# Talking-heads attention and a squared-ReLU FFN on one core: near copies ranked last, output matmuls in twos, and the left-over lines of the first batch as chunks of their own

## The chip, the cores and the metric

The kernel runs on one NeuronCore of a Trainium2 chip. The engines are named as in the profile: PE (TensorE, matrix multiply), DVE (VectorE), ACT (ScalarE), POOL (GpSimd) and SP (SyncE, which here only issues transfers). The metric is the device time of one execution in microseconds (us). All times before are of the kernel as it stood; the medians are over three runs.

## What is computed

Eight batches, twelve heads, 448 positions, head dimension 64. The scores of all heads are mixed across heads with a 12x12 matrix before the softmax, and the attention weights are mixed again with another one after it. The result, 3584 rows of 768, goes through an FFN with a squared ReLU.

```python
def _attn_ref(q, k, v, w_pre, w_post):              # q, k, v: (8, 12, 448, 64)
    scores = scale * np.matmul(q, k.transpose(0, 1, 3, 2))
    scores = np.einsum('bhij,hg->bgij', scores, w_pre)
    scores = scores - np.max(scores, axis=-1, keepdims=True)
    attn = np.exp(scores)
    attn = attn / (np.sum(attn, axis=-1, keepdims=True) + 1e-09)
    attn = np.einsum('bhij,hg->bgij', attn, w_post)
    return np.matmul(attn, v)

def _moe_ref(x, w_in, w_out):                       # x: (3584, 768), w_in: (768, 2048)
    h = np.maximum(x @ w_in, 0.0)
    return h * h @ w_out
...
    x = np.ascontiguousarray(attn_out.transpose(0, 2, 1, 3)).reshape(B * S, H * D)
    return _moe_ref(x=x, **moe_kwargs)
```

## The kernel before

**Order.** No loop issues the instructions directly. The program first describes its work as operations (`add`: an engine or a choice of engines with an assumed cost, a rank `pri`, a function that issues the instructions, what it depends on, a PSUM bank that it takes). `Planner.run` then plays the operations through an event list with those costs; each free engine takes the ready operation of lowest rank. The order that comes out is the program: each engine has a fixed list, and waits at its head for the semaphores of what that instruction needs. A wrong cost changes no result, only the order. The assumed costs are constants of the code, such as `NEAR` (L39), `load` (L498) and `first` (L1029). Ranks are counted in chunks: chunk n has rank n, and what must be ready for it has n minus some lead (`AHEAD`, L43). FFN operations have the rank `FILL` = 1e6, so they fill what attention leaves open. Where PE would stand idle early on, the planner inserts matmuls on a tile of zeros (`still`, L1183; the rule is in L234 with `IDLE_LOW`).

**One batch of attention.** The 448 query positions are cut into four blocks: r = 0 is the tail, the last 64 positions; r = 1, 2, 3 are three interleaved sets of 128 out of the first 384. Per batch:

1. q and k are transposed. In batches 0 and 1 PE does that (`t_qk`, L547). From batch 2 on (`x_piece`, L612) a *near copy* brings the heads next to each other (`pair_k`, `pair_q`, L616 to L620, into `kn` and `qn`; 3 + 3 copies for each half of the heads, on POOL or DVE as the planner chooses), and a DMA transpose issued by SP turns them into `kt` and `qz` (L623, L629). `kn` and `qn` exist once, so the second half's copies wait for the first half's transposes.
2. Scores (`score`, L679): one matmul of 448 columns for each head, two heads beside each other on half the rows of PE for r > 0, and one matmul for a pair of heads for the tail. They are evacuated by DVE or ACT (L485, L487, the `copy` helper) into one of two buffers `snat`.
3. A *relay* (`relayout`, L707) is a DMA issued by SP from `snat` to `sch`, which gathers 10 positions of 12 heads into 120 lines of 448: a *chunk*. There are 45 in a batch. The blocks' 128 positions are not a multiple of ten: eight lines of each are left over, and are put together with left-over lines of the block before it. `schl` is a buffer for one such chunk of 96 lines, whose first 24 come from the tail and whose other 72 from block 2.
4. For each chunk (`chunk`, L761): the mix (L801, PE, one matmul with the mixing matrix), the maximum (L812, DVE), the exponential with its sum (L815, ACT), the reciprocal for two chunks (L821, DVE), the second mixing matrix scaled by it (`wq`, L824, POOL), four matmuls that mix, transpose and normalise at once (`at`, L831, PE), and their evacuation into `atb` (L485 or L487).
5. When a block's chunks are through, `av` (L876) multiplies with v, and the result goes to `xt`, which holds the FFN input of two batches. The FFN runs on units of 128 or 256 positions (`unit`, L916): the first matmul (L933), ReLU (L947 on DVE, L951 on ACT), square (L954, POOL), the output matmuls (L972), their evacuation to `osb` (L989), the store (L996). An operation of the output matmuls is four of the 16 steps of a sum (L969).

**Batch 0 differs.** Block 1 comes first, as *direct* chunks: no score is stored and relayed. Instead DVE multiplies q with the fanned-out mixing matrix (`f_prep`, L790, into `osb`, not used by then), and six matmuls over the head pairs (L807) give the mixed scores at once. The places of the chunks are in `ORDER0` (L72): block 1's twelve whole chunks (7 to 18), its left-over chunk 6 (which includes the tail's lines), the tail's chunks 0 to 5, then 19 to 44. Chunk 19 is the one in `schl`, chunk 32 mixes left-over lines of blocks 2 and 3. `TAIL_FIRST` (L83) sets when the tail's scores are due. The tail's scores of batch 0 are stored in the second `snat` (L656), which block 3 uses later; L684 makes block 3's scores wait for the tail's relays.

**Queues.** SP issues all relays, all DMA transposes and nearly all stores, in order. POOL issues the loads (L350, L356, L361, L1068, L1074), between its `wq`, squares and near copies.

## Time and profile before

| | |
|---|---|
| median of three runs | 581.34 us (580.34 to 581.96) |
| the profiled execution | 582.53 us |
| its span, first to last instruction | 580.8 us |
| granted PE clock, mean | 0.997 |
| exponentials (L815, ACT) | x360, 641 ns each |
| maxima (L812, DVE) | x360, 610 ns each |
| first FFN matmul (L933), 128x256 and 128x128 | x1632, 164.3 us busy |
| output matmul (L972) | x912, 173.0 us busy |
| `wq` (L824, POOL) | x347, 123.6 us busy |
| near copies on DVE (L610) | 19 of k, 9.2 us; 16 of q, 6.5 us |
| near copies on POOL (L610) | 17 of k, 10.2 us; 20 of q, 10.5 us |

The profile is of one execution. Busy times of an engine are unions of its instructions' times; the ends of matmuls are modelled, so a matmul's own duration overlaps that of the next, and a busy PE is not PE at its peak. The page has 40 slices of 14.5 us: DVE is at eight tenths or more in all but the first and the last three, and the DMA engines are at nine tenths in the first four slices and at one or two tenths in the last.

### The profile page before, as it was taken

To read this page: it belongs to the slowest core of one execution; us is meant where nothing else is said; L and a number is where in the kernel's file an instruction comes from. 1 tells how busy PE (TensorE), PEld (TensorE's weight loads), DVE (VectorE), ACT (ScalarE), POOL (GpSimd) and SP (SyncE) were. 2 spreads that over 40 slices of the span, in tenths; PEclk is the share of its full clock that TensorE was granted. 3 is DMA by queue.
4 is the path that set the end of the run, shared out by engine and by line. 5 is a ranking of instruction groups with operands and counts; after the bars stand their busy time and mean duration, and the time that the engine had idled before them with its cause. 6 is when DMAs were issued, how large, how long until landed. Compare 5 with 4: busy or idle time off the path is not lost.

```text
span 580.8 us, 16782 instructions
## 1 busy us (share of the span) xinstructions
PE 566.0 (97%) x5820; PEld 406.4 (70%) x5820; DVE 507.6 (87%) x1124; ACT 452.4 (78%) x1198; POOL 323.0 (56%) x593
## 2 busy tenths in 40 slices
PE   7989999999999898999999999999999999999997
PEld 4667666776677576767668677767768676767785
DVE  7999998999989899989898998999899988988442
ACT  5789989789888876888897888889798888887200
POOL 8357356655665267635776357734677344645441
PEclk9999999999999999999999999999999999999999
DMA  9999849954897449764498649954297545322021
GB/s 136 217 186 220 164 114 197 159 146 125 155 157 169 136 120 182 158 133 122 92 204 144 158 142 143 199 131 133 76 201 160 153 139 113 118 75 80 2 56 54
DMA packets 131810, 80.90 MB, mean 139 GB/s; under 512 B 59298, under 2 KB 126732, under 8 KB 131724
## 3 DMA queue, kind: packets, MB, share of 16 engines
q1 hardware_dynamic: 84892, 56.99, 40.1%
q0 software_dynamic: 46784, 22.81, 30.3%
q8 instruction: 45, 0.74, 0.5%
q14 instruction: 41, 0.34, 0.2%
q10 hardware_dynamic: 48, 0.02, 0.0%
HBM read 45.61 MB, written 11.01 MB: 98 GB/s over the span
## 4 chain that ended last, share of the span: by engine, by line
PE 84%; DMA 5%; DVE 5%; POOL 3%; issue 2%; ACT 1%; DVEq 0%; SPq 0%; POOLq 0%
PE bank L933 24%; PE bank L972 22%; PE bank L831 12%; PE bank L801 10%; PE bank L876 6%; PE bank L679 6%; DMA ks<-in_k_dram 2%; DMA sch<-snat 2%; DVE mn L812 1%; PE bank L807 1%; DVE atb L485 1%; DMA qs<-in_q_dram 1%; POOL wq L824 1%; DVE snat L485 1%; POOL ks L361 1%
## 5 line engine op out<-in xcount | busy, mean ns | idle before, releaser
L815 ACT ACTIVATE es<-bank,mn 120x448 bf16<-120x448 f32 x360 | 228.0, 641 | 50.5 <-DVE mn L812 45.7
L824 POOL TENSOR_SCALAR wq<-wback,rc 120x120 bf16<-120x120 f32 (+1 forms) x347 | 123.6, 369 | 158.1 <-DVE rc L821 93.7
L812 DVE TENSOR_REDUCE mn<-bank 120x1 f32<-120x448 f32 x360 | 209.2, 610 | 2.0 <-PE bank L801 1.8
L972 PE MATMUL bank<-w,h 128*128 128x384 bf16 (+2 forms) x912 | 173.0, 323 | 0.0
L933 PE MATMUL bank<-xt,w 128*128 128x256 bf16 (+1 forms) x1632 | 164.3, 253 | 0.8 <-ACT es L815 0.7
L954 POOL TENSOR_TENSOR h<-hr 128x512 bf16<-128x512 f32 x112 | 116.5, 1041 | 66.0 <-DVE hr L947 37.0
L933 PEld LDWEIGHTS <-w 128*128 128x128 bf16 x1632 | 136.1, 98 | 24.5 <-issue 3.9
L831 PEld LDWEIGHTS <-es 120*112 120x112 bf16 (+1 forms) x1440 | 107.9, 130 | 31.9 <-ACT es L815 6.3
L485 DVE CAST atb<-bank 112x480 bf16<-112x480 f32 (+2 forms) x188 | 114.6, 617 | 13.6 <-PE bank L831 11.6
L831 PE MATMUL bank<-wq,es 120*112 120x120 bf16 (+1 forms) x1440 | 118.3, 217 | 5.8 <-POOL wq L824 3.5
L972 PEld LDWEIGHTS <-h 128*128 128x128 bf16 x912 | 85.8, 97 | 54.1 <-issue 2.1
L487 ACT CAST atb<-bank 112x480 bf16<-112x480 f32 (+3 forms) x196 | 103.0, 538 | 12.0 <-PE bank L831 10.1
L801 PE MATMUL bank<-sch,wmix 120*128 120x448 bf16 x339 | 107.0, 354 | 0.7 <-DVE atb L485 0.5
L485 DVE CAST snat<-bank 128x448 bf16<-128x448 f32 x152 | 88.8, 613 | 3.6 <-PE bank L679 1.5
L487 ACT CAST snat<-bank 128x448 bf16<-128x448 f32 x172 | 84.4, 543 | 4.6 <-PE bank L679 3.3
L815 ACT ACTIVATION_READ_ACCUMULATOR es<-bank,mn 120x1 f32 x360 | 74.1, 206 | 0.0
L947 DVE TENSOR_SCALAR hr<-bank 128x512 f32<-128x512 f32 x80 | 55.0, 688 | 18.5 <-PE bank L933 15.1
L801 PEld LDWEIGHTS <-wmix 120*128 120x128 bf16 (+1 forms) x347 | 30.9, 98 | 21.4 <-issue 12.7
L876 PE MATMUL bank<-atb,vs 112*64 112x192 bf16 (+3 forms) x864 | 40.4, 250 | 0.0
L679 PE MATMUL bank<-kt,qz 64*128 64x448 bf16 x276 | 39.0, 357 | 0.8 <-DVE hr L947 0.6
L876 PEld LDWEIGHTS <-vs 112*64 112x64 bf16 x864 | 36.4, 110 | 3.4 <-issue 2.5
L485 DVE COPY osb<-bank 128x384 f32<-128x384 f32 (+2 forms) x32 | 17.3, 541 | 21.3 <-PE bank L972 18.2
(72 smaller groups left out, 307.1 us busy)
## 6 DMA issues: line engine op xcount, KB each, us to landing
sch<-snat SPq DMA_DIRECT2D x324, 105.0 KB
out_dram<-osb SPq DMA_DIRECT2D x22, 360.0 KB
vs<-in_v_dram POOLq DMA_DIRECT2D x16, 336.0 KB, 8.3
ks<-in_k_dram POOLq DMA_DIRECT2D x14, 336.0 KB, 9.5
qs<-in_q_dram POOLq DMA_DIRECT2D x14, 288.0 KB, 9.9
w<-in_moe_w_in_dram POOLq DMA_DIRECT2D x6, 512.0 KB, 14.6
w<-in_moe_w_out_dram POOLq DMA_DIRECT2D x4, 768.0 KB, 19.6
out_dram<-osb SPq DMA_DIRECT2D x8, 192.0 KB
```

What stands on the lines that cost most here:

```text
L485: nc.vector.tensor_copy(out=out_, in_=in_)
L487: nc.scalar.copy(out=out_, in_=in_)
L679: nc.tensor.matmul(slot[:, 0:S], lhsT=lhsT, rhs=kt[i][half, :, at_, :], start=True, stop=True)
L801: nc.tensor.matmul(slot[:, 0:S], lhsT=wm[0:rows, :], rhs=src[0:rows, :], start=True, stop=True,)
L812: nc.vector.tensor_reduce(out=mn[i][0:rows, :], in_=slots[mk][0:rows, 0:S], axis=AX.X, op=ALU.min)
L815: nc.scalar.activation(out=es[i][0:rows, 0:S], in_=slots[mk][0:rows, 0:S], func=ACT.Exp, scale=-1.0, bias=mn[i][0:rows, 0:1], accum_out=sm ...
L824: nc.gpsimd.tensor_scalar(out=wq[i][0:rows, :, 0:ns], in0=back[0:rows, :, 0:ns], scalar1=rc[i // 2][0:rows, i % 2:i % 2 + 1], scalar2=1.0, ...
L831: nc.tensor.matmul(slot[0:P_KEYS, jb * H * ns:(jb + 1) * H * ns], lhsT=es[i][0:rows, jb * P_KEYS:(jb + 1) * P_KEYS], rhs=wq[i][0:rows, :, ...
L876: nc.tensor.matmul(v_[64 * hh:64 * hh + 64, i, 0:x1 - x0], lhsT=vs[:, 2 * c2 + hh, jb, :], rhs=atb[half][:, jb, 2 * c2 + hh, x0:x1], start ...
L933: nc.tensor.matmul(slot[:, j * w:(j + 1) * w], lhsT=w1[c2][:, (f0 + j) * 128:(f0 + j + 1) * 128], rhs=xt[:, c2, a:z], start=(c2 == 0), sto ...
L954: nc.gpsimd.tensor_tensor(out=h2_[:, f0:f0 + nf, 0:w], in0=hr[gi % 2][:, :].rearrange("p (f c) -> p f c", f=nf), in1=hr[gi % 2][:, :].rear ...
L972: nc.tensor.matmul(slot[:, 0:c1 - c0], lhsT=h2_[:, ft, mt * 128:(mt + 1) * 128], rhs=w2[:, ft, c0:c1], start=(ft == 0), stop=(ft == FT - 1),)
```

## The change

Five things, and constants of the plan.

- *Near copies rank last.* `pair_k` and `pair_q` get the rank 2e6, behind everything else, and other assumed costs (POOL 640 ns where it was 1000, DVE 480 where it was 270).
- *Output matmuls in twos.* An operation of L972 is two of the 16 steps (`OSTEP`), not four, and costs half in the plan.
- *Left-over lines of batch 0 apart.* Chunk 6 keeps the left-over lines of block 1 and the tail, chunk 19 now holds those of block 2 and the tail and becomes direct like chunk 6, ahead of the tail's chunks; chunk 32 holds block 3's alone (96 lines). `schl` is no longer used in batch 0. 14 direct chunks, not 13.
- *Tail scores of batch 0 in `xt`*, in the half that batch 1 fills later: block 3's scores no longer wait for the tail's relays. Instead batch 1's evacuations to `xt` wait for them (`old += relay_of[0]`), and batch 1's k and q slots wait for the tail scores' matmuls (`used`). The tail's scores are due by their own chunk's place, not by `TAIL_FIRST`.
- *AV earlier in the program of batch 0*: blocks 0 and 2 are given to `av` behind their last whole chunk (`C0[1] - 1`, `C0[3] - 1`).
- Constants: `AHEAD` 7.4 to 7.0, `IDLE_LOW` 0.55 to 0.62, a load's issue 750 to 830 ns, and the assumed times of the first loads (k 48 to 52, q 36 to 42, tail 24 to 30 ns a row).

```diff
 NSLOT = 2
-NEAR, TURN_SP = {"POOL": 1000, "DVE": 270}, 1500
+NEAR, TURN_SP = {"POOL": 640, "DVE": 480}, 1500
 PIECE = NPAIR // 2
...
 NSCH = 11
-AHEAD = 7.4
+AHEAD = 7.0
 FIFO = 50
-IDLE_NS, IDLE_COLS, IDLE_FROM, IDLE_END, IDLE_LOW = 112, 256, 1300, 130000, 0.55
+IDLE_NS, IDLE_COLS, IDLE_FROM, IDLE_END, IDLE_LOW = 112, 256, 1300, 130000, 0.62
 SPELL, PHASE, DROP, RISE = 3413, 1700, 0.4, 0.8
...
 LATER = 2
+NEAR_LAST = 2e6
+OSTEP = 2
 GS, ONE = [(0, 1, 2)], [(0,), (1,), (2,)]
...
 UNITS0 = [(0, 128), (128, 256), (256, 384), (384, 640), (640, 896)]
-ORDER0 = [*range(C0[1] + 1, C0[2]), C0[1], *range(C0[1]), *range(C0[2], NCHUNK)]
+EARLY = 6
+ORDER0 = [*range(C0[1] + 1, C0[2]), C0[1], C0[2], *range(EARLY), *range(C0[2] + 1, C0[3]), *range(EARLY, C0[1]), *range(C0[3], NCHUNK)]
 NQW = 4
...
 TAIL0, Q0 = 19, 0.7
-TAIL_FIRST = 8
 
...
             deps = list(deps) + [loads[-7]]
-        op = add("POOL", 750, pri, fn, deps, lat=850)
+        op = add("POOL", 830, pri, fn, deps, lat=850)
         done = pl.moved("LOAD", rows, each[0], each[1], 0, [op], 1500)
...
         i = 2 * b + piece - NSLOT
-        far = prep_op + [m_op[n] for n in direct] if b == 1 else []
+        far = prep_op + [m_op[n] for n in direct] + [score_ops[0, 0, p] for p in range(NPAIR)] if b == 1 else []
         return far + [score_ops[i // 2, NJ, PIECE * (i % 2) + x] for x in range(PIECE)] if i >= 0 else []
...
         ck = [
-            add(NEAR, 0, pri, lambda eng, a=a: pair_k(eng, a), [k_in[b, g], tk_op.get(2 * b + g - 1)], lat=80)
+            add(NEAR, 0, NEAR_LAST, lambda eng, a=a: pair_k(eng, a), [k_in[b, g], tk_op.get(2 * b + g - 1)], lat=80)
             for a in range(PIECE)
...
         cq = [
-            add(NEAR, 0, pri, lambda eng, a=a: pair_q(eng, a), [q_in[b, g], tq_op.get(2 * b + g - 1)], lat=80)
+            add(NEAR, 0, NEAR_LAST, lambda eng, a=a: pair_q(eng, a), [q_in[b, g], tq_op.get(2 * b + g - 1)], lat=80)
             for a in range(PIECE)
...
     def store_of(b, r):
-        return snat[1 if b == 0 and r == 0 else r % 2]
+        return xt[:, :, S:W2B] if b == 0 and r == 0 else snat[r % 2]
 
...
     def is_direct(b, c):
-        return b == 0 and C0[1] <= c < C0[2]
+        return b == 0 and C0[1] <= c <= C0[2]
 
...
 
-        first = TAIL_FIRST if b == 0 and r == 0 else C0[r]
+        first = min(place_of(b, c) for c in range(C0[r], (C0 + [NCHUNK])[r + 1]) if not is_direct(b, c)) - b * NCHUNK
         pri = b * NCHUNK + first - AHEAD - 0.6 - (0.7 if r == 0 else 1.4) * (NPAIR - p)
         n = b * (NJ + 1) + r - 2
-        old = list(relay_of.get(n if n != 1 else 0, [])) if n else []
+        old = list(relay_of.get(n, [])) if n > 1 else []
         ins = [op for p_ in group for op in ready[b, p_][r]] + ([ready_tail[b, p]] if r == 0 else [])
...
             parts = [(blk, 0, KC, sn[2 * CI * cc:2 * CI * (cc + 1), 0:NPAIR, :])]
+        elif b == 0 and cc == 0:
+            parts = [(blk, 0, 96, sn[120:P, :, :])]
         elif cc == 0:
...
             relay_of.setdefault(of, []).append(move(n, pri, ns, deps + old, src_of[n][r0:r1, :], srcs, lat))
-        if r == 0 and cc == 5:
+        if r == 0 and cc == 5 and b > 0:
             here.append(move(
...
             return [(half, base + CI * (cc - 1), 0, CI)]
+        if b == 0 and r > 1:
+            return [(0, rest + 62, 0, 2), (1, 120, 2, 8)] if r == 2 else [(1, P_ROWS + 120, 0, 8)]
         return [
...
         r, cc = block_of(c)
-        rows = 96 if c == C0[2] else KC
+        rows = 96 if c == C0[2 if b else NJ] else KC
         ns = rows // H
...
             for lo, hi, first, x, s0, step, w in (
-                ([(64 * x_, 64 * x_ + 64, 0, zt, P - 8 + x_, 2, 2) for x_ in range(2)] if cc == 0 else []) +
+                ([(64 * x_, 64 * x_ + 64, 0, zt, P - 8 + 4 * (r - 1) + x_, 2, 2) for x_ in range(2)] if cc == 0 else []) +
                 [(0, P, PIECE * i_, qz[i_], CI * (cc - 1) if cc else P_ROWS - 8, 1, CI if cc else 8) for i_ in range(2)]
...
                     o = 2 if w == 8 else 0
-                    src_ = x[lo:hi, 0, :, s0:s0 + w] if size < NPAIR else x[lo:hi, :, s0:s0 + step * (w - 1) + 1:step]
+                    src_ = x[lo:hi, r - 1, :, s0:s0 + w] if size < NPAIR else x[lo:hi, :, s0:s0 + step * (w - 1) + 1:step]
                     (nc.vector if eng == "DVE" else nc.gpsimd).tensor_tensor(
...
         old = []
+        if b == 1:
+            old += relay_of[0]
         if b >= 2:
...
                 key = ("f", ix, "o", mt, nt)
-                for f0 in range(0, FT, 4):
+                for f0 in range(0, FT, OSTEP):
                     def mms(slot, f0=f0, mt=mt, c0=c0, c1=c1):
-                        for ft in range(f0, f0 + 4):
+                        for ft in range(f0, f0 + OSTEP):
                             nc.tensor.matmul(
...
                     if f0 == 0:
-                        prev = add("PE", 12 + (c1 - c0) * 5 // 3, fill + 20 + 4 * mt + 2 * nt, keep(key, mms),
-                                   [prev] + sq_op[ix][0:4 // nf] + w2_in[0:1 if ix < SOON else 4], lat=0, bank=key)
+                        prev = add("PE", (12 + (c1 - c0) * 5 // 3) * OSTEP / 4, fill + 20 + 4 * mt + 2 * nt, keep(key, mms),
+                                   [prev] + sq_op[ix][0:max(1, OSTEP // nf)] + w2_in[0:1 if ix < SOON else 4], lat=0, bank=key)
                     else:
-                        prev = add("PE", 12 + (c1 - c0) * 5 // 3, FILL, lambda key=key, mms=mms: mms(slots[key]), [prev, w2_in[f0 // 4]] + sq_op[ix][0:(f0 + 4) // nf], lat=0)
+                        prev = add("PE", (12 + (c1 - c0) * 5 // 3) * OSTEP / 4, FILL, lambda key=key, mms=mms: mms(slots[key]), [prev, w2_in[f0 // 4]] + sq_op[ix][0:(f0 + OSTEP + nf - 1) // nf], lat=0)
                     o_op[ix].append(prev)
...
         if what[0] == "k":
-            k_in[0, what[1]] = first(us, 28, 48)
+            k_in[0, what[1]] = first(us, 28, 52)
         elif what[0] == "a":
...
         elif what[0] == "q":
-            q_in[0, what[1]] = first(us, 32, 36)
+            q_in[0, what[1]] = first(us, 32, 42)
         elif what[0] == "t":
-            tails0.append(first(us, 24, 24))
+            tails0.append(first(us, 24, 30))
     tail_in[0] = add("TAIL", 0, 0, lambda: None, tails0, lat=0)
...
                 unit(0, 0)
-            if c == C0[2]:
+            if c == C0[1] - 1:
                 for gs in ONE:
                     av(0, 0, gs, P_ROWS, XA)
-            if c == C0[3]:
+            if c == C0[3] - 1:
                 for gs in ONE:
```

## The prediction

> **What bounds the kernel now.** I read the busy times of the page first, then the busy time by stage, then what ended TensorE's (PE's) waits, and last the order of time around the longest of them.
>
> ```profile
> span 580.8 us, 16782 instructions
> PE 566.0 (97%) x5820; PEld 406.4 (70%) x5820; DVE 507.6 (87%) x1124; ACT 452.4 (78%) x1198; POOL 323.0 (56%) x593
> ```
>
> PE is busy 97% of the span, so the time is PE's work plus the little that it idles: 580.8 − 566.0 = 14.8 us. The stages tell where that is (columns: length, then busy us of PE, weight load, DVE, ACT, POOL, then clock, DMA share, GB/s):
>
> ```profile
> 16.00:33.00 17.00, 16.93 (x117) 11.97 (x116) 16.78 (x48) 11.95 (x32) 4.93 (x11) 1.00 1.05 208
> 33.00:55.00 22.00, 20.38 (x333) 15.30 (x332) 20.55 (x50) 20.65 (x56) 17.30 (x30) 1.00 1.25 205
> 55.00:68.00 13.00, 11.26 (x163) 7.41 (x162) 13.00 (x32) 12.05 (x35) 4.05 (x11) 1.00 0.98 184
> ...
> 150.00:240.00 90.00, 86.38 (x868) 61.14 (x863) 83.13 (x178) 72.31 (x196) 56.16 (x103) 1.00 0.88 159
> 240.00:540.00 300.00, 299.98 (x3007) 216.53 (x3005) 271.93 (x589) 253.52 (x675) 169.53 (x318) 1.00 0.63 134
> 540.00:581.00 41.00, 37.02 (x319) 27.72 (x316) 13.61 (x24) 2.30 (x6) 12.10 (x13) 1.00 0.14 40
> ```
>
> From 240 to 540 PE never idles: there, a reordering moves the end only if it changes PE's own work. Up to 68 us it is VectorE (DVE) that is full (16.78 of 17.00, 13.00 of 13.00), and the FFN has little to give PE. So time can be won in three places: the first 68 us, 150 to 240 us (3.6 us of PE idle), and the last 4 us, a closing evacuation and store that the edit leaves alone. What ended PE's waits after the first minute:
>
> ```profile
> PE bank L831 <- POOL wq L824: 1.6, 2, 0.9
> PE bank L831 <- DVE osb L485: 1.6, 1, 1.6
> PE bank L933 <- ACT es L815: 0.7, 1, 0.7
> PE bank L679 <- DVE hr L947: 0.6, 1, 0.6
> ```
>
> The 0.6 and the 0.7 are one event. In order of time:
>
> ```profile
> 225.36 0.60 POOL L610 COPY kn<-ks 112x512 bf16<-112x512 bf16 x1
> 226.03 2.38 DVE L610 COPY kn<-ks 112x512 bf16<-112x512 bf16 x1
> 227.20 1.05 POOL L954 TENSOR_TENSOR h<-hr 128x512 bf16<-128x512 f32 x1
> 229.45 0.37 PE L679 MATMUL bank<-kt,qz 64*128 64x448 bf16 x2 [0.63 <-DVE hr L947]
> 231.36 1.47 PE L933 MATMUL bank<-xt,w 128*128 128x256 bf16 x12 [0.69 <-ACT es L815]
> ```
>
> One near copy took 2.38 us on DVE, where the median of its kind is 0.295 (the tile's view), while GpSimd (POOL) worked without a break from 225.36 to 228.25; the DVE work queued behind it then held PE.
>
> **The change, part by part.** The sum is made against the profiled execution: 582.53 us, of which the span is 580.8. The median of the runs is 581.34, so 1.19 is taken off at the end.
>
> *One more direct chunk in batch 0.* Block 2's left-over lines become a direct chunk: six matmuls for one. Twelve direct matmuls took 2.44 us (at 29.96) and six took 1.30 (at 33.20), so 0.19 each: PE gains 5 × 0.19 = 0.95. DVE gets four more preparations (L790): two of 64x144 at 0.300 and two of 128x288 at 0.295, together 1.19. Both fall where PE (16.93 of 17.00) and DVE are full. Against it, one evacuation piece of `atb` falls away and 21 fewer KB are relayed. Bounds: 0 if a hole swallows it, +1.2 if DVE pays all. I take +0.9, near the full price, as that stage has no holes. Five more standing matmuls (39 to 44) fill holes of PE by construction: 0. The cover is a wait that is there anyway; without it they would cost 5 × 0.11 = 0.6 (half of the 0.213 of one at the half clock of the start).
>
> *Left-over lines apart, tail scores in `xt`.* Block 3's scores no longer wait for the relays of the tail, which held the same buffer; block 2 is complete after its twelfth relayed chunk, one chunk before the mixed chunk with block 3. So the AV matmuls of the second unit, which started at 66.05, can start a chunk earlier: 42 maxima began between 17.7 and 69.9, so (69.9 − 17.7) / 41 = 1.27 us. What it can win are PE's holes from 55 to 68: 13.00 − 11.26 = 1.74, and the five standing matmuls just before that AV (0.65). Bounds: 0, if DVE, full there, sets the pace anyway, and −2.4. I take −1.2, one chunk.
>
> *The start.* Load costs are raised in the plan, so the order now puts scores between the transposes of q, where PE idled 0.67 and 1.07 us for q. Block 2's twelve score matmuls all stand ahead of the first direct chunk (eight before) and five of the six tail scores behind it. The first maximum still needs all of q and its preparations. Bounds −1.7 and 0; I take −0.4, as the loads set the pace.
>
> *Near copies rank last.* In the built order DVE has 19 of them, 35 before; POOL 53, 37 before. The 35 on DVE took 9.2 + 6.5 = 15.7 us (groups of L610), against 35 × 0.29 = 10.2 at the median: some 5.5 us are such blocked time, and 16/35 of it goes. POOL gets 8 × 0.61 + 8 × 0.55 = 9.3 us more, and stays under 60%. Each copy's transposes still stand 12 and more chunks ahead of the scores that need them, so lateness costs nothing. Worth to PE: the event at 226 cost 0.63 + 0.20 + 0.69 = 1.52; DVE's other delays are hidden under FFN matmuls. Bounds −2.5 (with half of DVE's 5.5 × 16/35 = 2.5 reaching PE early, at 150 to 240) and +1.0 (two POOL waits of the 0.9 kind return before `wq`). I take −1.5.
> [...]
>
> *FFN output in pieces of two.* The matmuls are the same, 880 of 384 columns in the group with the most forms; a filler lasts 0.33 us rather than 0.65. Entries into the scores' half-row mode go from 70 to 71 in the built order, so switching costs nothing new. Mixes followed at once by their `at` (the pair in which PE waits for `wq`) go from 40 to 32, and the pieces fill such gaps. The holes it can reach: 0.91 at 79.21, 0.45 at 167.91, 1.58 at 198.07. Bounds −2.9 and +0.7 (a delay of 0.1 at each of seven more score-to-filler changes). The 1.58 hangs on an output store that DVE and ACT wait for, which no piece of PE shortens; I take −1.0.
>
> *The constants* (AHEAD, IDLE_LOW, load costs) act through the order above: 0.
>
> Sum: 0.9 − 1.2 − 0.4 − 1.5 − 1.0 = −3.2; 582.53 − 3.2 = 579.3 for a profiled run, and 579.3 − 1.2 = 578.1 against the median.
>
> **The rivals.**
> *Nothing is won* (0.14). DVE paces the first 68 us with as much work as before, the w2 loads keep the first output matmuls back to 80.5 us whatever comes before, and the holes at 79, 168, 198 and 229 reappear elsewhere, as such holes belong to any plan that is off by a microsecond. For it: DVE at 13.00 of 13.00. Against it: the near copy at 226 has a cause that the change addresses. Left are 0.9 of cost and about 1.3 of gain: 580.9.
> *The relays of batch 0 come late: slower* (0.21). Before, all six tail scores were evacuated ahead of the first maximum, their relays issued from 17.6, 0.8 us apart, for a first use at 32.23. Now the last tail score stands behind the second pair of `at`, which ended at 24.66 + 0.59 = 25.25; the six relays wait for its evacuation, to about 26, and block 2's twelve queue behind them on SyncE, to about 26 + 18 × 0.8 = 40.4. The DMA engines are full here (share 1.05, 1.25). The queue's view gives the relays' pace: from 22 to 31, beside the w1 loads, 467 packets of theirs, and from 32 to 35, with those loads landed, 643 (columns: packets, MB, share of the engines):
>
> ```profile
> q1 hardware_dynamic: 467, 0.39, 16.8%
> ...
> q1 hardware_dynamic: 643, 0.53, 53.5%
> ```
>
> A relay is 120 lines, so 2.3 us there and 0.56 us here. The tail's own relays are still in time: the first, behind loads for 3.4 us as before (issued 17.57, no packet from 17 to 21), lands near 26 + 3.4 + 2.3 = 31.7, and its use moves one direct chunk on, to 32.23 + 1.27 = 33.5. But they take the fast stretch from 32 to 35 that was block 2's, and block 2's then fall among batch 1's loads of q and k, issued from 32.89. Block 2 is needed from 33.5 + 6 × 1.27 = 41. It decides when the pace among those loads falls to that beside w1: twelve times 2.3 us from 35 end at 62.6, against a use of the last at 41 + 12 × 1.27 = 56. If half of that delay of 6 stands as a hole of ACT, DVE and PE together (the FFN matmuls of the first unit fill some), 3 us are lost, and with the direct chunk and half of the other gains the run ends at 581.34 + 3 + 0.9 − 2.0 = 583.2. For it: the load of the engines. Against it: without relays beside them the w1 loads end sooner, by about 0.39 MB at 211 GB/s, 1.8 us, and the bytes are the same.
> *It does more than said*: all holes within reach close (start −1.7, AV −2.4, near copies −2.5, pieces −2.9) and the direct chunk costs 0.9: −8.6, 572.7. It is the low end of the forecast's case.
>
> **How the numbers follow.** What a measurement of this kernel can tell is about 0.3%, 1.7 us: faster is below 579.6, slower above 583.1. The forecast's case, the closing of more holes in it, holds 0.65, with its own range 573 to 580.5; almost all of it counts as faster. Nothing won: 0.14. Late relays: 0.21, nearly all of it above 583.1, as its price is open upwards. So faster 0.64, same 0.17 (with the upper edge of the forecast's case and the lower one of the late relays), slower 0.19. The range of 573 to 585 takes in both other cases and leaves out the closing of every hole and a hole of over 5 us.
>
> **What would show it.** Right: no near copy over 1.5 us on DVE with a PE wait behind it around 226; the second unit's AV before 65.5; PE idle from 150 to 240 under 2 us; output matmuls in twos between an `es` and its `at`. The direct chunk shows as 84 direct matmuls, and as a first relayed mix later than 32.2. Wrong: a hole of PE, DVE and ACT together between 33 and 60, ended by a relay into `sch` (the late relays); PE idle as large as before with new releasers (nothing won); a wait of `at` for `wq` behind near copies on POOL. If PE idles again after 240, a premise has fallen that all the cases share.

## The result, and the profile after

| | before | after |
|---|---|---|
| median, eight runs each beside each other | 582.70 us (580.34 to 585.48) | 578.40 us (577.92 to 580.14) |
| after / before | | 0.9913, 95% interval 0.9887 to 0.9939 |
| the profiled execution, its span | 582.53, 580.8 | 577.99, 576.2 |

The recorded ratio times 582.7 is a gain of 5.1 us (3.6 to 6.6), where 3.2 was forecast; the forecast's own ratio, 578.1 / 581.34 = 0.9944, lies just above the interval. (581.34 was the median of the first three of the eight runs before.) The recorded ratio is not the quotient of the two medians, which is 0.9926, a gain of 4.3; this text goes by recorded ratios throughout. The page of the changed kernel:

```profile
span 576.2 us, 16829 instructions
PE 565.1 (98%) x5830; PEld 407.5 (71%) x5830; DVE 510.2 (89%) x1124; ACT 445.9 (77%) x1185; POOL 329.4 (57%) x609
```

Its stages (columns as in the prediction: length, busy us of PE, weight load, DVE, ACT, POOL, clock, DMA share, GB/s):

```profile
12.00:16.00 4.00, 3.83 (x35) 1.97 (x34) 3.99 (x14) 4.00 (x11) 2.67 (x5) 1.00 1.37 198
...
33.00:55.00 22.00, 21.48 (x334) 16.28 (x332) 20.80 (x52) 20.25 (x58) 16.39 (x29) 1.00 1.23 199
55.00:68.00 13.00, 12.38 (x198) 9.24 (x198) 13.00 (x33) 11.57 (x34) 5.00 (x12) 1.00 0.95 179
...
90.00:150.00 60.00, 59.08 (x628) 43.24 (x625) 56.10 (x123) 47.88 (x128) 34.31 (x68) 1.00 0.76 145
150.00:240.00 90.00, 88.87 (x894) 63.40 (x895) 86.98 (x183) 73.34 (x199) 59.36 (x108) 1.00 0.88 163
240.00:540.00 300.00, 298.98 (x3036) 217.73 (x3033) 272.84 (x585) 251.15 (x668) 173.45 (x328) 1.00 0.65 135
```

The start of the kernel before, the same stage:

```profile
12.00:16.00 4.00, 3.88 (x30) 2.10 (x29) 3.64 (x13) 3.61 (x9) 2.57 (x5) 0.57 1.39 202
```

Length less PE's busy time gives its idle time in each stage of the two profiled executions:

| PE idle, us | 0 to 33 | 33 to 90 | 90 to 150 | 150 to 240 | 240 to 540 | 540 to the end | all |
|---|---|---|---|---|---|---|---|
| before | 3.0 | 4.3 | 0.1 | 3.6 | 0.0 | 3.8 | 14.8 |
| after | 2.9 | 1.2 | 0.9 | 1.1 | 1.0 | 3.9 | 11.1 |

So 5.5 us of holes went, 3.0 in batch 0's attention and FFN start and 2.5 between 150 and 240, and 1.8 came back elsewhere. Idle falls by 3.7 and the span by 4.6. The last 0.9 is in busy time. The clock from 12 to 16 was 0.57 before and is 1.00 now, which is worth an estimated (1.00 − 0.57) × 4 = 1.7 us of PE's work; against it stand the five added direct matmuls, 0.9. All of this is of one execution of each kernel.

What ended PE's waits in the changed kernel (columns: us in total, times, longest):

```profile
PE bank L807 <- DVE snat L487: 2.0, 2, 1.1
PE bank L1191 <- DVE still L369: 1.1, 1, 1.1
```

The waits of `at` for `wq` (L824 before, L830 now) are gone from its lines; before, there were five between 33 and 68 us alone:

```profile
PE bank L831 <- POOL wq L824: 2.6, 5, 0.8
```

In order of time, what the prediction asked to see in batch 0; first the kernel before, then the changed one:

```profile
32.23 0.35 PE L801 MATMUL bank<-sch,wmix 120*128 120x448 bf16 x1
...
66.05 1.53 PE L876 MATMUL bank<-atb,vs 112*64 112x128 bf16 x48
```

```profile
30.77 1.35 PE L813 MATMUL bank<-kt,osb 128*120 128x448 bf16 x6
...
35.29 0.35 PE L807 MATMUL bank<-sch,wmix 120*128 120x448 bf16 x1
...
62.76 1.53 PE L882 MATMUL bank<-atb,vs 112*64 112x128 bf16 x48
...
77.17 0.49 PE L980 MATMUL bank<-w,h 128*128 128x384 bf16 x2
```

The added direct chunk stands at 30.77. The first relayed mix is 3.1 later than before (32.23), and yet the AV of the second unit is 3.3 earlier (66.05) and the first output matmul too (80.50), which goes out as a piece of two. And the event that was to vanish, a near copy on DVE kept out by POOL, is still there, at another place:

```profile
166.25 2.90 DVE L612 COPY qn<-qs 128x384 bf16<-128x384 bf16 x1
...
166.95 2.04 POOL L962 TENSOR_TENSOR h<-hr 128x512 bf16<-128x512 f32 x2
...
169.08 0.60 DVE L487 CAST snat<-bank 128x448 bf16<-128x448 f32 x1
...
169.73 0.92 PE L807 MATMUL bank<-sch,wmix 120*128 120x448 bf16 x3 [1.11 <-DVE snat L487]
```

The copy ends at 169.15, 0.16 after POOL's squares (168.99), as the one at 226 did before; the evacuation behind it on DVE is late, and PE waits 1.11. DVE's near copies are 19 now (35 before), three of them over 1 us (five before). Together they take 7.1 + 5.2 = 12.3 us. Less 19 × 0.29 = 5.5, as the prediction counted, that leaves 6.8 us in which they are kept out, where it was 5.5 before: there are fewer copies on DVE, but no less of this time.

### The profile page after: what moved, and what is told of

The parts are those of the page before. It is cut to its first block, busy times and chain, and to the rows that moved or that the text cites. A ratio compares the mean times of both kernels' runs of the same rounds, so it can differ in the third digit from the quotient of the medians.

```text
span 576.2 us, 16829 instructions
## 1 busy us (share of the span) xinstructions
PE 565.1 (98%) x5830; PEld 407.5 (71%) x5830; DVE 510.2 (89%) x1124; ACT 445.9 (77%) x1185; POOL 329.4 (57%) x609
## 4 chain that ended last, share of the span: by engine, by line
PE 87%; DVE 6%; DMA 3%; ACT 2%; issue 1%; POOL 0%; DVEq 0%; ACTq 0%; POOLq 0%
PE bank L980 24%; PE bank L941 23%; PE bank L837 12%; PE bank L807 11%; PE bank L882 7%; PE bank L681 6%; DMA sch<-snat 3%; PE bank L813 2%; DVE mn L818 1%; DVE atb L487 1%; DVE snat L487 1%; PE bank L1191 1%; ACT es L821 1%; DVE qn L612 1%; ACT snat L489 0%
## 5 line engine op out<-in xcount | busy, mean ns | idle before, releaser
L830 POOL TENSOR_SCALAR wq<-wback,rc 120x120 bf16<-120x120 f32 (+1 forms) x346 | 123.0, 367 | 148.4 <-DVE rc L827 90.3
L980 PE MATMUL bank<-w,h 128*128 128x384 bf16 (+2 forms) x912 | 184.1, 323 | 0.0
L837 PEld LDWEIGHTS <-es 120*112 120x112 bf16 (+1 forms) x1440 | 110.9, 129 | 27.7 <-ACT es L821 3.7
L837 PE MATMUL bank<-wq,es 120*112 120x120 bf16 (+1 forms) x1440 | 120.8, 217 | 0.5 <-ACT es L821 0.2
L980 PEld LDWEIGHTS <-h 128*128 128x128 bf16 x912 | 83.7, 98 | 51.7 <-issue 5.2
L487 DVE CAST atb<-bank 112x480 bf16<-112x480 f32 (+3 forms) x184 | 112.9, 622 | 7.8 <-PE bank L837 4.9
L489 ACT CAST atb<-bank 112x480 bf16<-112x480 f32 (+3 forms) x199 | 103.8, 537 | 19.1 <-PE bank L837 18.3
L807 PE MATMUL bank<-sch,wmix 120*128 120x448 bf16 (+1 forms) x339 | 108.2, 354 | 2.6 <-DVE snat L487 2.0
L489 ACT CAST snat<-bank 128x448 bf16<-128x448 f32 x165 | 81.8, 546 | 7.7 <-PE bank L681 7.2
L955 DVE TENSOR_SCALAR hr<-bank 128x512 f32<-128x512 f32 x75 | 51.6, 688 | 19.3 <-PE bank L941 16.9
L487 DVE COPY osb<-bank 128x384 f32<-128x384 f32 (+2 forms) x42 | 22.8, 543 | 16.8 <-PE bank L980 16.2
```

The source lines that it names most:

```text
L487: nc.vector.tensor_copy(out=out_, in_=in_)
L489: nc.scalar.copy(out=out_, in_=in_)
L807: nc.tensor.matmul(slot[:, 0:S], lhsT=wm[0:rows, :], rhs=src[0:rows, :], start=True, stop=True,)
L830: nc.gpsimd.tensor_scalar(out=wq[i][0:rows, :, 0:ns], in0=back[0:rows, :, 0:ns], scalar1=rc[i // 2][0:rows, i % 2:i % 2 + 1], scalar2=1.0, ...
L837: nc.tensor.matmul(slot[0:P_KEYS, jb * H * ns:(jb + 1) * H * ns], lhsT=es[i][0:rows, jb * P_KEYS:(jb + 1) * P_KEYS], rhs=wq[i][0:rows, :, ...
L980: nc.tensor.matmul(slot[:, 0:c1 - c0], lhsT=h2_[:, ft, mt * 128:(mt + 1) * 128], rhs=w2[:, ft, c0:c1], start=(ft == 0), stop=(ft == FT - 1),)
```

## The experiments

The kernels were timed in three sessions, each on another chip, in five rounds against the kernel before. "Undone" starts from the changed kernel, "alone" from the kernel before. The medians of the kernel before in the three sessions were 584.75, 584.60 and 583.41, so ratios are compared, not times. The changed kernel itself was not run again beside them: its ratio is that of the first table.

| | ratio to before, 95% | in us of 582.7 |
|---|---|---|
| changed kernel | 0.9913 (0.9887 to 0.9939) | −5.1 |
| near copies undone | 0.9968 (0.9942 to 0.9994) | −1.9 |
| pieces of two undone | 0.9941 (0.9916 to 0.9965) | −3.4 |
| batch 0 undone | 0.9970 (0.9936 to 1.0003) | −1.7 |
| constants undone | 0.9996 (0.9965 to 1.0028) | −0.2 |
| near copies alone | 0.9977 (0.9943 to 1.0011) | −1.3 |
| pieces of two alone | 0.9961 (0.9934 to 0.9987) | −2.3 |
| batch 0 alone | 1.0115 (1.0064 to 1.0165) | +6.7 |
| batch 0 with the constants | 0.9973 (0.9946 to 1.0000) | −1.6 |
| near copies on POOL only | 1.0010 (0.9985 to 1.0035) | +0.6 |
| near copies on DVE only | 1.0328 (1.0291 to 1.0364) | +19.1 |
| near copies on POOL and ACT | 0.9991 (0.9966 to 1.0016) | −0.5 |
| `AHEAD` 7.1 | 0.9924 (0.9899 to 0.9950) | −4.4 |

The recorded ratios differ from the quotients of the medians by up to some 0.002. With these quotients pieces of two undone is at 0.9927, where the changed kernel is at 0.9926, and `AHEAD` 7.1 at 0.9916. So a price of 1 to 2 us is not told from 0 by the times alone.

### Each part taken out of the change

Near copies with their old rank and costs:

```diff
-NEAR, TURN_SP = {"POOL": 640, "DVE": 480}, 1500
+NEAR, TURN_SP = {"POOL": 1000, "DVE": 270}, 1500
-            add(NEAR, 0, NEAR_LAST, lambda eng, a=a: pair_k(eng, a), [...], lat=80)
+            add(NEAR, 0, pri, lambda eng, a=a: pair_k(eng, a), [...], lat=80)
```

> The changed kernel with the near copies as before (their old rank and assumed costs). Theory 'parts': the near copies are worth 1.5 us of the 5.1, so this run stands at about 0.994 of the kernel before (579.5 where the changed one has 578.4), DVE has near copies of over 1 us again, and PE idles 1 to 2 us more between 150 and 240 us. Rival 'plan': no part has a price of its own, any other order of the same work moves the time by 1 to 2 us either way; then it may also be faster than 578.4, and its PE holes lie elsewhere than behind near copies.

Measured: 582.39 us (581.39 to 584.89), 0.9968. The part is worth (0.9968 − 0.9913) × 582.7 = 3.2 us where it stands, twice the 1.5 forecast; the two intervals do not overlap. PE idles 2.5 from 150 to 240, 1.1 with the part: that is 1.4 of it.

Output matmuls in fours:

```diff
-OSTEP = 2
+OSTEP = 4
```

> The changed kernel with output matmuls in pieces of four again. 'Parts': 1.0 us is lost, about 0.993 (579.4), and matmuls that PE waits for behind a maximum or wq show 1 us more idle. If the pieces are the main part of the gain (the forecast undersized them, bound 2.9), 0.996 to 0.997 (581). 'Plan': within 2 us of 578.4 on either side.

Measured: 580.49 us (579.72 to 581.70), 0.9941: 1.6 us, with overlapping intervals, so a loss is not shown. Here the idle time misleads: this kernel's PE idles 9.5 us, less than the changed kernel's 11.1, and its span is 2.1 longer. Of the 1.6 us that it idles less, 1.4 lie in the first 33 us, where PE works more slowly: of the first 16 us it is busy for 14.54 with 139 matmuls, in the changed kernel for 13.10 with 143. Besides, the ends of matmuls are modelled, so part of a wait hides in busy time. A better account is the time from each matmul's start to the next one's, less its columns at 0.417 ns, an estimate from the starts in the traces (256-column FFN matmuls in a row start 109 ns apart, 384-column ones 162 to 163, so 128 columns cost 53 to 54, 0.414 to 0.422 ns each; two AV matmuls of 256 columns beside each other start 109 ns behind the two before them, so half of that):

| time beyond the columns, us | before | pieces of two undone | changed |
|---|---|---|---|
| all matmuls | 57.9 | 53.9 | 51.8 |
| up to 16 us | 7.6 | 7.7 | 6.8 |
| from 150 to 240 us | 11.1 | 9.6 | 7.8 |
| between a mix and an `at` behind it, 90 to 535 us | 2.5 (31 of them) | 1.8 (33) | 0.2 (28) |
| between two matmuls of `at`, 90 to 535 us | 5.2 | 5.0 | 4.2 |

All of the 2.1 between the last two is there (53.9 − 51.8), but 0.8 of it lies in the first 16 us, which this part does not touch. Another 1.6 stands just where the prediction put the pieces' use, between a mix and its `at`; other pairs gain and lose the rest. That the pieces are what closed this gap is not shown. With pieces of two undone, three waits (at 165, 213 and 215 us) make 1.6 of the 1.8. Before, one wait of 1.76 behind the mix at 196 makes most of the 2.5. The same sum is 0.4 in a kernel with pieces of four (batch 0 with the constants, below), and 1.8 and 1.3 in two kernels with pieces of two (pieces alone, batch 0 undone).

Batch 0 as it was, all else changed (the edits to `ORDER0`, `store_of`, `is_direct`, the parts and ranks of the left-over chunks and the place of `av` are taken back):

```diff
-ORDER0 = [*range(C0[1] + 1, C0[2]), C0[1], C0[2], *range(EARLY), ...]
+ORDER0 = [*range(C0[1] + 1, C0[2]), C0[1], *range(C0[1]), *range(C0[2], NCHUNK)]
...
-        return xt[:, :, S:W2B] if b == 0 and r == 0 else snat[r % 2]
+        return snat[1 if b == 0 and r == 0 else r % 2]
-        return b == 0 and C0[1] <= c <= C0[2]
+        return b == 0 and C0[1] <= c < C0[2]
```

> The changed kernel without its part in batch 0 (left-over chunks, tail scores in snat, AV places as before), with near copies last, pieces of two and the new constants. 'Parts': the batch 0 part was forecast at -1.2 - 0.4 + 0.9 = -0.7, so about 0.9925 (579.1), and PE idle from 0 to 68 us rises by about 1. If batch 0 holds most of the gain, 0.997 (581). If the direct chunk costs more than it wins, faster than the changed kernel, below 0.990 (577.5).

Measured: 582.44 us (579.72 to 586.68), 0.9970. The part is worth 3.3 us, though its interval just touches that of the changed kernel; the profiled execution took 585.19. Its stages in batch 0:

```profile
33.00:55.00 22.00, 20.77 (x351) 16.04 (x349) 20.68 (x48) 19.40 (x56) 17.48 (x30) 1.00 1.27 208
55.00:68.00 13.00, 11.44 (x132) 7.12 (x132) 12.57 (x32) 11.65 (x33) 3.55 (x10) 1.00 0.95 180
```

The holes are back (1.23 and 1.56), and over the run there are six waits of `at` for `wq`, 2.8 us.

The constants as they were:

```diff
-AHEAD = 7.0
+AHEAD = 7.4
-IDLE_NS, IDLE_COLS, IDLE_FROM, IDLE_END, IDLE_LOW = 112, 256, 1300, 130000, 0.62
+IDLE_NS, IDLE_COLS, IDLE_FROM, IDLE_END, IDLE_LOW = 112, 256, 1300, 130000, 0.55
-        op = add("POOL", 830, pri, fn, deps, lat=850)
+        op = add("POOL", 750, pri, fn, deps, lat=850)
...
-            k_in[0, what[1]] = first(us, 28, 52)
+            k_in[0, what[1]] = first(us, 28, 48)
...
```

> The changed kernel with the old AHEAD, IDLE_LOW, load cost and first load times. 'Parts': the constants were put at 0 of their own, with -0.4 for the start, so 0.992 (578.8), PE idle in the first 16 us larger by 0.4. 'Plan': anything within 2 us of 578.4; a loss of over 1.5 us would say that the costs in the plan were the change.

Measured: 583.81 us (582.34 to 586.97), 0.9996. Taking the constants back takes nearly the whole gain away. Edits costed at nothing were, by the ratios, the dearest single part to lose, 4.8 us; which of the constants it is was not tried.

The four losses (differences of the ratios, by 582.7) sum to 3.2 + 1.6 + 3.3 + 4.8 = 12.9, against a gain of 5.1: what each part costs to lose does not add up to the gain.

### Each part alone

Near copies alone (the first diff above the other way round, on the kernel before):

> The kernel before with the near copies' new rank and costs alone. 'Parts': -1.5 us, about 0.997, and no near copy on DVE of over 2 us ahead of a PE wait. After the first four runs (each part undone alone lost 2 to 5 us of the 5) the rival is 'together': the parts win only jointly, since one hole that is left lets the others reappear; then this run is at 0.998 to 1.002, and its PE idle is as large as before, 14 to 15 us.

Measured: 583.82 us (580.64 to 588.90), 0.9977; no gain is shown. Its profiled execution was its longest, 588.9, and shows one way in which a run gets long. In order of time:

```profile
169.94 3.60 DVE L611 COPY qn<-qs 128x384 bf16<-128x384 bf16 x1
...
171.35 2.03 POOL L955 TENSOR_TENSOR h<-hr 128x512 bf16<-128x512 f32 x2
...
173.46 1.20 DVE L486 CAST atb<-bank 112x480 bf16<-112x480 f32 x2
...
174.15 0.35 PE L802 MATMUL bank<-sch,wmix 120*128 120x448 bf16 x1 [2.09 <-DVE atb L486]
```

POOL's instructions follow each other from 169.65 to 173.38, and one DVE copy is kept out through all of them. PE waits 2.09. Its stages just there, and just after:

```profile
172.00:175.40 3.40, 1.31 (x13) 1.05 (x11) 3.40 (x5) 0.18 (x1) 1.39 (x2) 1.00 1.23 109
175.50:178.90 3.40, 3.40 (x15) 1.35 (x14) 3.40 (x9) 3.40 (x10) 2.50 (x4) 0.50 1.48 181
```

For 3.4 us PE was busy for 1.31, and for the next 3.4 its clock is halved (0.50): by estimate up to 1.7 us more, behind the 2.09 of waiting.

Pieces alone (`OSTEP` = 2 on the kernel before):

> The kernel before with output matmuls in twos alone. 'Parts': -1.0 us, about 0.998. 'Together': 0.998 to 1.003, PE idle of 13 to 15 us; the holes ahead of the first output matmul at 80 us (some 8 us up to there) stay in both theories, as there is nothing to cut in two before it.

Measured: 582.04 us (580.48 to 584.80), 0.9961, a gain of 2.3 (0.8 to 3.8), shown. PE idle from 150 to 240 is 0.1, where it was 3.6, but 2.4 come back after 240.

Batch 0 alone, with the old constants:

> The kernel before with the new batch 0 alone (left-over chunks apart, one direct, tail scores in xt, AV earlier), old near rank, pieces and constants. 'Parts': -0.7 us, about 0.999. If this part carries the run-to-run spread (the kernel before lies between 580.5 and 590.5, the changed one without this part between 579.7 and 586.7, with it within 2 us), its times spread by under 4 us and its median is 0.993 to 0.996. 'Together': 0.998 to 1.002.

Measured: 592.34 us (587.18 to 593.82), 1.0115: 6.7 us *slower*. The largest wait of PE, and the clock around it:

```profile
PE bank L681 <- DMA kt<-kn: 3.9, 1, 3.9
```

```profile
118.00:122.00 4.00, 0.30 (x2) 0.23 (x3) 0.35 (x2) 0.00 (x0) 0.32 (x1) 1.00 1.48 103
122.40:129.20 6.80, 5.55 (x26) 3.00 (x25) 3.24 (x9) 3.75 (x10) 1.82 (x5) 0.50 0.52 154
```

Near copies of the next half stood at the heads of DVE's and POOL's lists, 4.7 us each, for a DMA transpose that had to free `kn`; all engines stood, and then the clock was halved for 6.8 us. So most of the loss seen here is one event at 118 us (3.9 of waiting and up to 3.4 of clock), behind near copies, and not in batch 0 itself. Why that transpose came so late with these costs was not tried.

Batch 0 with its constants, near copies and pieces as before:

> The kernel before with the new batch 0 and the new constants, without the near rank and the pieces of two. Alone the new batch 0 was 1.0115, and the constants with the other two parts but the old batch 0 were 0.997. Theory 'batch 0 and the load costs are one part': PE idles 1.0 to 1.6 us from 33 to 90 us (4.3 before, 3.8 with the new batch 0 and old costs) and the time is 0.993 to 0.997. Rival (the pieces or the near rank are what mends the new batch 0): 1.0 or above, with 3 us or more idle there.

Measured: 581.07 us (579.93 to 586.37), 0.9973, a gain of 1.6 at the interval's edge.

```profile
33.00:55.00 22.00, 21.48 (x330) 16.04 (x331) 21.09 (x53) 19.91 (x55) 17.27 (x31) 1.00 1.17 190
55.00:68.00 13.00, 12.37 (x198) 9.10 (x196) 12.71 (x32) 11.55 (x34) 4.52 (x11) 1.00 1.00 187
```

PE's busy time here is the changed kernel's to 0.01. The traces of all these kernels let the two parts be told apart, by the time from the first `at` to the AV of the second unit:

| batch 0 / constants | kernel | first `at` | AV | between |
|---|---|---|---|---|
| old / old | before | 21.96 | 66.05 | 44.09 |
| new / old | batch 0 alone | 22.07 | 65.38 | 43.31 |
| new / old | constants undone | 21.04 | 64.36 | 43.32 |
| old / new | batch 0 undone | 22.18 | 67.33 | 45.15 |
| new / new | batch 0 with the constants | 22.18 | 63.64 | 41.46 |
| new / new | pieces of two undone | 22.13 | 63.58 | 41.45 |
| new / new | near copies undone | 21.89 | 63.35 | 41.46 |
| new / new | changed kernel | 21.30 | 62.76 | 41.46 |

The new batch 0 by itself makes the stretch 0.8 shorter, the constants by themselves 1.1 longer, both together 2.6 shorter. It repeats to 0.01 whatever the other parts are, so it is in the order, not in the run. They are one edit: an order and the costs that it was planned with. Taken so, the three parts by themselves sum to −1.3 − 2.3 − 1.6 = −5.2, the whole gain; their intervals, ±1.5 to ±2 each, allow that to be chance.

### Is it the near copies on DVE that POOL keeps out?

The prediction put the near part's gain down to copies on DVE kept out by POOL. Three kernels change the engines that may take them, with the changed rank. All copies on POOL (the two lambdas that issue a copy then name the one engine):

```diff
-NEAR, TURN_SP = {"POOL": 640, "DVE": 480}, 1500
+NEAR, TURN_SP = {"POOL": 640}, 1500
...
```

> The changed kernel with all 72 near copies on POOL. Theory 'lock' (a copy on DVE from one SBUF tile to another stands until POOL, busy without a break, pauses): no copy of over 1 us is left, since none is on DVE; the wait of the mix for a score evacuation behind such a copy (1.1 us at 169.7 in the changed kernel) goes, and the time is 0.987 to 0.991 of the kernel before. Rival 'POOL becomes the bound': 19 copies of 0.6 more on POOL make at wait for wq, 1 us or more in total, and the time is 0.992 or above. Reshuffling alone was worth 1.3 us (the lead of 7.1), so only beyond that does the time itself decide; the waits decide first.

Measured: 583.98 us (583.03 to 585.88), 1.0010. No DVE copy is left to be kept out, and the kernel is 5.7 us slower than the changed one. PE's waits, and the longest in order of time:

```profile
PE bank L837 <- POOL wq L830: 1.7, 2, 1.5
```

```profile
215.44 0.71 PE L837 MATMUL bank<-wq,es 120*112 120x120 bf16 x8 [1.47 <-POOL wq L830]
```

That `wq` had itself waited 2.04 for DVE's `rc`, so it isn't the copies on POOL ahead of it that made it late.

All copies on DVE:

```diff
-NEAR, TURN_SP = {"POOL": 640, "DVE": 480}, 1500
+NEAR, TURN_SP = {"DVE": 480}, 1500
...
```

> The changed kernel with all 72 near copies on DVE. 'Lock': they take far more than 72 x 0.29 = 21 us, 35 us or more, with six or more over 1 us, and the time is 0.993 to 0.997, with PE waiting for DVE work behind them. Rival (a copy on DVE at 0.29 us is cheaper than on POOL at 0.6, and long ones were chance): under 25 us in total, and the time as the changed kernel's.

Measured: 602.07 us (600.22 to 604.94), 1.0328. The copies themselves (busy us, mean ns, idle before) and PE's waits:

```profile
L612 DVE COPY kn<-ks 112x512 bf16<-112x512 bf16 x36 | 15.2, 438 | 0.1
L612 DVE COPY qn<-qs 128x384 bf16<-128x384 bf16 x36 | 11.9, 347 | 0.0
```

```profile
PE bank L837 <- POOL wq L830: 6.4, 7, 2.1
PE bank L807 <- DMA sch<-snat: 4.5, 7, 1.8
```

Being kept out cost DVE 27.1 − 72 × 0.29 = 6 us, not 19, and three copies took over 1 us. What else there is in the trace is lateness: ranked last on an engine that is busy for 86% of the span, the copies are put off. The last k copy starts at 475.7, in the changed kernel at 443.4. PE waits for relays and for `wq`, and idles 22.2 us in all. On top of that its granted clock is 0.96 from 150 to 240 and 0.99 from 240 to 540, where the changed kernel has 1.00 in both.

None on DVE, 22 of them on ACT:

```diff
-NEAR, TURN_SP = {"POOL": 640, "DVE": 480}, 1500
+NEAR, TURN_SP = {"POOL": 640, "ACT": 560}, 1500
...
-        (nc.gpsimd if eng == "POOL" else nc.vector).tensor_copy(out=out_, in_=in_)
+        nc.gpsimd.tensor_copy(out=out_, in_=in_) if eng == "POOL" else nc.scalar.copy(out=out_, in_=in_)
```

> The changed kernel with near copies on POOL or ACT, none on DVE. 'Lock': ACT's copies hold their duration whatever POOL does (largest within 1.5 times the median), no wait of PE behind them, and the time is 0.987 to 0.991. Rival 'any engine that gets the copies queues its evacuations behind them': 0.992 or above, with waits of PE for ACT.

Measured: 582.48 us (581.31 to 585.67), 0.9991. The copies of k on ACT last 606 to 669 ns: none is kept out. Yet it is 4.5 us slower than the changed kernel, and PE waits 1.4 for relays, which it does not in the changed kernel.

So taking the copies off DVE, twice, did not bring the price of their being kept out. The time in which DVE's copies are kept out points the same way: near copies undone has 34 of them in 8.9 + 6.5 = 15.4 us, less 34 × 0.29 that is 5.5, and the changed kernel 6.8. In these executions, what the near part wins is therefore not that time, and no run here isolates what it is instead.

### What a reshuffle alone is worth

```diff
-AHEAD = 7.0
+AHEAD = 7.1
```

> The changed kernel with AHEAD 7.1 in place of 7.0: relays and scores due 0.1 chunk sooner, which has no mechanism that could be worth more than 0.1 us; it only reshuffles ties of the plan. 'Parts': 0.991, the changed kernel's time. 'Plan': 1 to 3 us slower (0.993 to 0.996), PE holes in other places than the changed kernel's: then a part's price of 1 us can't be told from the reshuffle that any edit brings.

Measured: 579.70 us (578.26 to 581.07), 0.9924. A lead moved by a tenth of a chunk changes the ratio by 0.0011, 0.6 us, within the intervals. Holes of PE move (2.1 us of idle after 240, 1.0 in the changed kernel), their sum hardly (10.7, 11.1). By the recorded ratio, none of the kernels tried was faster than the changed one. (The expectation of the copies on POOL, above, counts 1.3 us for this edit, from the medians of two sessions.)

## Why the prediction was right, and where not

*The sign and the place* held: PE's idle time went in the two stretches that were named, 33 to 68 (with what follows to 90) and 150 to 240. The marks seen: 84 direct matmuls, the first relayed mix after 32.2, the AV before 65.5, PE idle from 150 to 240 under 2 us, output matmuls in twos. The mark of the near copies holds only to the letter: none is kept out at 226, but one is at 166. That the total came out near is in part luck, since its terms did not hold one by one.

*Left-over lines apart (−1.2)* and *the constants (0)*: the step that failed is "act through the order above: 0". The AV moved by 2.6 against the first `at`, not by one chunk of 1.27; the new batch 0 alone makes it 0.8, and the rest appears only with the constants. Together with the direct chunk the forecast for both was 0.9 − 1.2 + 0 = −0.3. Measured by themselves they give −1.6, and PE idle from 33 to 90 falls by 3.0. The mistake was to give the costs a term of their own: the order is solved from them, and the new batch 0 with the old costs is another kernel, 6.7 us slower than the one before, largely by the one event at 118 us.

*The direct chunk (+0.9)*: six matmuls in 1.35 us, where 1.30 was read; what it costs the end was not tried by itself.

*The start (−0.4)*: not shown. Four kernels with the new batch 0 and constants, whose order up to there is not touched by near copies or output matmuls, have their first `at` at 21.30, 21.89, 22.13 and 22.18 (before: 21.96). What differs is how fast PE works up to there. Near copies undone has a granted clock of 0.65 from 12 to 16, and the two latest have PE busy for 14.54 and 14.47 of the first 16 us with 139 matmuls, the changed kernel for 13.10 with 143. The 0.7 by which the changed kernel's profile starts earlier lies within that scatter.

*Near copies last (−1.5)*: −3.2 in place, −1.3 alone with an interval that holds 0. The size is off, and so is the mechanism given for it: of 5.5 us in which DVE's copies were kept out, 16/35 was to go, and 6.8 are there now. The 2.90 us copy at 166 is the same event as the one at 226, its price 1.11 where that was 1.52. Nor does "lateness costs nothing" hold everywhere: with all copies on DVE the last k copy starts 32 us later, and the kernel is 19 us slower than the one before. In the bounds, two waits of 0.9 are 1.8, not the +1.0 that the prediction gives.

*Pieces of two (−1.0)*: −2.3 alone, shown and inside its bounds; −1.6 in place, not clear of the noise. The mechanism is not shown: the time between a mix and its `at` falls from 1.8 to 0.2 us in place, but it is 1.8 with pieces alone and 0.4 in a kernel with pieces of four. The 1.58 at 198 that "no piece shortens" is gone, but a wait that the profile also puts down to an output store (DVE 1.27, ahead of an evacuation into `snat`; PE 0.92 behind it) stands at 96.

*The rivals.* Late relays: not seen. The first relayed mix came at 35.29, later than the 33.5 reckoned, and no hole of PE, DVE and ACT followed; PE idles 0.52 in the 22 us from 33. Nothing is won: no, although its sentence that such holes reappear elsewhere is true of 1.8 us.

*The shared premise*, that PE doesn't idle after 240: it idles 1.0 there, at 300 and 335. The premise was also weaker than it looked. Counted from start to start, PE spent 19.6 us beyond its columns from 240 to 540 before, with an idle time of 0.0.

What stays open: why copies on POOL alone or on POOL and ACT lose 4.5 to 5.7 us, what the near copies' rank wins, and which constant matters. That the parts together gain 5.1, where near copies and pieces with the constants give 1.7 (batch 0 undone) and batch 0 with the constants 1.6, needs no further cause: with the old batch 0 the new constants cost 1.1 (first `at` to AV), and the 0.7 that remain lie within the intervals of these two, ±1.9 and ±1.6.

## What to carry to other kernels

Where a planner makes the order, an assumed cost is part of the edit that it was tuned with: price the pair, and try an edit with the old costs before calling the costs nothing. Count what PE loses from start to start of its matmuls rather than as idle time: with modelled ends, each wait above shows as some 0.16 us less idle than it cost (0.62 for 0.78 at 213 with pieces of two undone), and slow work at the start can hide waits (with pieces of two undone PE idles 1.4 less up to 33 us, and is busy for 14.54 of the first 16 where the changed kernel is for 13.10). Before a part's price is put down to a mechanism, look whether the time that the mechanism names went. And look at the clock behind a hole in which PE is mostly idle for a few microseconds: behind 1.31 us of work in 3.40 (172, near copies alone) it was 0.50 for 3.4 us.

## What the runs showed of the hardware

*The clock.* A granted clock of 0.50 stood for 3.41 us from 12.18 in the kernel before, for 3.4 from 175.5 (near copies alone), for 3.4 from 250.6 (batch 0 undone) and for 6.8 from 122.4 (batch 0 alone). Several windows at 0.50 came behind one in which PE was little busy: 1.31 of 3.40 us at 172, 0.46 of 2.90 at 234 (near copies alone), 1.43 of 3.50 at 247 (batch 0 undone). One came behind 1.97 of 3.00 at 36 (near copies alone). The longest waits in the first three were 2.09, 2.75 and 1.96. PE was 16 to 66% busy in these four stretches; no threshold follows from them. The granted clock of the profile does not tell all: in the kernel before it reads 1.00 from 0 to 4, while 256-column matmuls (`still`) start 213 ns apart up to 4.45 us and 109 from 5.65 on. Of the runs of batch 0 with the constants, the two at a mean granted clock of 0.993 and 0.991 took 583.92 and 586.37 us, and the ten at 0.997 and above 579.9 to 582.4. It is not the whole spread, though: batch 0 undone took 586.13 at 1.000.

*Near copies on DVE beside POOL.* A near copy on DVE took 3.60 us (169.94, near copies alone) through five POOL instructions in a row (169.65 to 173.38), without a turn between them; the median of such a copy in the changed kernel is 0.28. It ended at 173.54, 0.16 us after the last of them. So did the copy at 226 before (228.41, POOL 228.25) and the one at 166 in the changed kernel (169.15, POOL 168.99). That POOL keeps the copy out is read from these three; no run shows by what. The copy at 166.25 in the changed kernel shows one thing more: for its first 0.7 us POOL was not computing but issuing a load (from 166.10 to 166.93), and the copy did not end then either; the copy at 226 before stood through such an issue too (226.36 to 227.17).
